# Attention with a learned position bias and a gated MLP, float32: in the bias stage, VectorE and ScalarE share the relu blocks and the copies out of PSUM, and GpSimd makes none

## The chip, the core and the metric

One core of a Trainium2 chip runs the whole program. The metric is the device time of one execution in microseconds (us). The engines are TensorE (PE in the rows; PEld is its weight load), VectorE (DVE), ScalarE (ACT), GpSimd (POOL), and SyncE (SP), which issues most DMAs. A "q" behind an engine's name is its sequencer, which issues and waits.

## What is computed

The reference is an attention block (4 batches, 8 heads, 576 positions, head dimension 64) whose scores get a bias from a small network on relative positions, followed by a gated MLP (512 to 2048 to 512) over the 2304 tokens:

```
pos = np.arange(S)
psi_rel = np.log1p(np.abs(pos[:, None] - pos[None, :]))
psi_i = np.log1p(np.maximum(pos[:, None], 1.0))
x = (psi_rel / psi_i)[..., None]
h = np.maximum(x @ w1 + b1, 0.0)
bias = h @ w2
scores = scale * np.matmul(q, k.transpose(0, 1, 3, 2)) + bias.transpose(2, 0, 1)[None]
...
g = h * np.tanh(sp)
return (g @ w_out)
```

Only the bias stage is touched: `x`, `h` and `bias` above.

## The kernel before

The program has three stages: the position bias (about the first 73 us of the trace), the attention over 16 head pairs with 5 row chunks each, and the MLP.

**The bias stage.** The bias of a row i and a column j depends on |i - j| and on i alone, so for 16 rows at a time the kernel makes a table over the distance and lets a DMA lay it out as rows. It does so in 36 turns, in the order of the list `ts` (lines 417 and 433); "turn 5" below is the sixth of that list. Each turn has

- four relu blocks `ht` (`make_h`, lines 448 to 463): `max(at + bb, 0)` over 128 partitions (4 rows x 32 hidden units) and n distances, n from 304 to 576. `maker`, a table of the engine of each block, is filled by a planner (lines 429 to 446): it keeps a sum of what each engine has spent and gives a block to the engine that would be done first, by prices per element;
- matmuls with `w2t` into a PSUM tile `bps` of 1024 columns (lines 488 to 492); there are two such tiles, so the matmuls of a turn need the tile of two turns earlier to be copied out;
- two scaled copies out of PSUM into `bt` (`evac`, lines 465 to 475): the left part, read backwards (`ps[:, left:0:-1]`), and the right part (`ps[:, :right]`). Both start at the low columns of the tile. Both are done by ScalarE here (lines 469 and 470);
- a DMA from `bt` to the bias table in DRAM, issued by SyncE (line 475). `bt` has eight buffers.

The loop (lines 482 to 512) makes the blocks of turn idx + 2, then issues the matmuls of turn idx, then the copies of turn idx - 1. GpSimd's blocks are made two turns further ahead (line 485). The engines work in the order of their instructions, so whatever stands behind a waiting instruction on the same engine waits too. ScalarE and VectorE also do the first steps of the attention in between (`SOFT_AT`): scores, add_bias (line 230, VectorE), exps (line 240, ScalarE) and norm (lines 246 and 247 on VectorE, 250 on GpSimd) of steps 0 and 1 behind turns 18 and 27, and splits of k and q (lines 174 and 179) at turns 9 and 12. GpSimd issues the 1.2 MB loads `qkhi` (line 169); line 511 is the second of these.

**Behind the stage.** The bias chunks are read back by `load_bias` (lines 182 to 193). The last one waits for the DRAM writes of the last turns; step 4 of the attention adds it (line 230).

Of the kernel before, what the change touches and what calls it, by code (L numbers as in the profile page):

```python
# [11 lines left out]
ALU = mybir.AluOpType  # L12
# [34 lines left out]
def kernel(ctx: ExitStack, tc, qk, v, wb, w2, w_in, w_out, psia, psi4, rinv, eye, out):  # L47
    nc = tc.nc
    pe, dve, act, pool, sp = nc.tensor, nc.vector, nc.scalar, nc.gpsimd, nc.sync
# [107 lines left out]
    def load_raw(i):  # L157
        hp, b = divmod(i, B)
        raw = rawp.tile([P, QW], F32, name="rawqk")
        sp.dma_start(out=raw[0:64], in_=qk[b, hp, 0:64, :QW])  # L160
        sp.dma_start(out=raw[64:128], in_=qk[b, hp, 64:128, QW:])
        vt = vp.tile([P, 2, 5, D], F32, name="vt")
        sp.dma_start(out=vt, in_=v[b, hp].rearrange("p (h c d) -> p h c d", h=2, c=5))
        qk_raw[i], v_t[i] = raw, vt

    def load_hi(i):
        hp, b = divmod(i, B)
        hi = hip.tile([P, 2 * QW], F32R, name="qkhi")
        pool.dma_start(out=hi, in_=qk[b, hp])
        qk_hi[i] = hi  # L170

    def split_k(i):
        kl = qk_hi[i][64:128, QW:]
        dve.tensor_tensor(kl, qk_raw[i][64:128], kl.bitcast(F32), op=ALU.subtract)

    def split_q(i):

        lo = q_los[i % 2]
        dve.tensor_tensor(lo[0:64], qk_raw.pop(i)[0:64], qk_hi[i][0:64, :QW].bitcast(F32), op=ALU.subtract)  # L179
        q_lo[i] = lo  # L180

    def load_bias(hp, c):
        h0, h1 = 2 * hp, 2 * hp + 1
        rows = P if c < 4 else 64
        src = bias_d[c][:, :rows * PITCH].rearrange("h (i j) -> h i j", j=PITCH)[:, :, PAD:PAD + S]
        t = bias_t[hp, c] = biasp.tile([P, 2 * S if c < 4 else S], F32, name=f"bias{c}")
        if c < 4:
            sp.dma_start(out=t[:, 0:S], in_=src[h0])
            sp.dma_start(out=t[:, S + 64:], in_=src[h1, :, 0:512])
            sp.dma_start(out=t[:, S:S + 64], in_=src[h1, :, 512:S])  # L190
        else:
            for r in range(2):
                sp.dma_start(out=t[r * 64:r * 64 + 64], in_=src[h0 + r])
# [48 lines left out]
    def norm(n):  # L242
        c = steps[n][1]
        pt, m = live[n]
        k = 2 if c < 4 else 1
        dve.tensor_scalar(m[:, 4:4 + k], m[:, 2:2 + k], 1e-9, None, op0=ALU.add)  # L246
        dve.reciprocal(m[:, 4:4 + k], m[:, 4:4 + k])  # L247
        if c < 4:
            pv = pt.rearrange("p (h s) -> p h s", h=2)
            pool.tensor_tensor(pv, pv, m[:, 4:6].unsqueeze(2).to_broadcast([P, 2, S]), op=ALU.mult)  # L250
        else:
            pool.tensor_tensor(pt[:, S:640], pt[:, 512:S], m[:, 4:5].to_broadcast([P, 64]), op=ALU.mult)
            pool.tensor_tensor(pt[:, 0:S], pt[:, 0:S], m[:, 4:5].to_broadcast([P, S]), op=ALU.mult)
# [149 lines left out]
    at = bc.tile([P, S], F32, name="at")  # L403
# [3 lines left out]
    rinv_t = bc.tile([P, S // 16], F32, name="rinv_t")  # L407
    bb = bc.tile([P, S // 4], F32, name="bb")
# [13 lines left out]
    def reach(t):  # L422

        left, right = 16 * t + 15, S - 16 * t
        n = max(left + 1, right)
        return left, right, n + n % 2


    spent = {"v": 0.0, "a": 0.0, "g": 1.1}
    maker = {}  # L430
    SOFT_AT = (18, 27, 35)
    BIAS_AT = (12, 20, 24, 32, 36)
    for idx, t in enumerate(ts):
        spent["a"] += 1.15 + (1.6 if idx in SOFT_AT else 0.0)
        spent["v"] += (1.8 if idx in SOFT_AT else 0.0) + (1.4 if idx in (9, 12) else 0.0)
        spent["g"] += 2.1 if idx - 4 in SOFT_AT else 0.0
        n = reach(t)[2]
        price = {"v": 0.13 + 0.00052 * n, "a": 0.26 + 0.00071 * n}
        if idx >= 3:
            price["g"] = 0.2 + 0.0046 * n  # L440
        for cg in (3, 2, 1, 0):
            e = min(price, key=lambda k: spent[k] + price[k])
            spent[e] += price[e]
            maker[idx, cg] = e
            if e == "g":
                del price["g"]

    def make_h(idx, engines):
        if idx >= NB:
            return  # L450
        n = reach(ts[idx])[2]
        for cg in range(4):
            e = maker[idx, cg]
            if e not in engines:
                continue
            ht = hpool.tile([P, S], F32, name="ht")
            k = 4 * ts[idx] + cg
            if e == "a":
                act.activation(ht[:, :n], at[:, :n], AF.Relu, bias=bb[:, k:k + 1])
            else:  # L460
                eng = dve if e == "v" else pool
                eng.tensor_scalar(ht[:, :n], at[:, :n], bb[:, k:k + 1], 0.0, op0=ALU.add, op1=ALU.max)  # L462
            h_t[idx, cg] = ht

    def evac(t):
        ps = bps_t.pop(t)
        bt = bo.tile([P, NW], F32, name="bt")
        left, right, _ = reach(t)
        act.mul(bt[:, :left], ps[:, left:0:-1], rinv_t[:, t:t + 1])
        act.mul(bt[:, left:], ps[:, :right], rinv_t[:, t:t + 1])  # L470

        c = t // 8
        a = (16 * t - P * c) * PITCH + PAD - 15
        dst = bias_d[c][:, a:a + 16 * (PITCH + 1)].rearrange("h (i j) -> i h j", j=PITCH + 1)
        sp.dma_start(out=dst[:, :, :NW], in_=bt)

    make_h(0, "va")
    make_h(1, "va")
    make_h(3, "g")
    load_hi(0)  # L480
    sp.dma_start(out=ident, in_=eye)
    for idx in range(NB + 2):
        if idx < NB:
            t = ts[idx]
            make_h(idx + 4, "g")
            make_h(idx + 2, "va")
            n = reach(t)[2]
            ps = bps.tile([P, 1024], F32, name="bps")
            for a in range(0, n, 512):
                for cg in range(4):  # L490
                    pe.matmul(ps[cg * 32:cg * 32 + 32, a:min(a + 512, n)], w2t,  # L491
                              h_t[idx, cg][:, a:min(a + 512, n)], start=True, stop=True)
            bps_t[t] = ps
        if 1 <= idx <= NB:
            evac(ts[idx - 1])
        if idx == 1:
            load_raw(0)
        if idx == 9:
            split_k(0)
        if idx == 12:  # L500
            split_q(0)
        if idx in BIAS_AT:
            load_bias(0, ORDER[BIAS_AT.index(idx)])
        for lag, do in enumerate((scores, add_bias, exps)):
            if idx - lag in SOFT_AT:
                do(SOFT_AT.index(idx - lag))
        if idx - 4 in SOFT_AT[:-1]:
            norm(SOFT_AT.index(idx - 4))
        if idx == 14:
            load_raw(1)  # L510
        if idx == 18:
            load_hi(1)
# [204 lines left out]
```

## Time and profile before

| what | us |
|---|---|
| median of 3 runs (784.4 to 784.8) | 784.63 |
| the profiled execution, its own time | 784.46 |
| span of that execution's trace | 782.7 |
| VectorE busy in the span | 616.9 |
| ScalarE busy in the span | 451.2 |
| GpSimd busy in the span | 327.4 |
| TensorE busy in the span | 729.7 |

The span is the time between the first and the last instruction of the program that was recorded; 1.8 us of the execution's own time lie around it. A busy share is an average over stages with different limits, so the rows below are taken from the bias stage by stretches of the span (us from its start). In rows, `out<-in` gives the tiles, then partitions x elements, `xN` the number of instructions merged into the row, and a bracket the idle time before it and what ended that. The duration of an instruction is somewhat longer than the distance to the next start on its engine, since two overlap at their ends; the distance is called its slot below.

### The profile page before, as it was taken

Reading aid. Unit: us, or ns where it says so; the run is one execution under the profiler, and the core shown is the slowest. Engines: PE = TensorE matmul, PEld = TensorE weight load, DVE = VectorE, ACT = ScalarE, POOL = GpSimd, SP = SyncE. Lnnn points to the kernel's source line nnn. Section 1 sums busy time; section 2 is a strip of 40 time slices with the busy share of each in tenths; the row PEclk is TensorE's granted clock in tenths of the full one; section 3 lists DMA queues with packets and bytes.
Section 4 is the critical chain, followed back from the end, with each engine's and each line's share of the span. In section 5 each row is a group of like instructions: output and inputs, shape, how many; then the busy total and the mean of one; then the engine's idle time right before and its main releaser. Section 6 shows DMA issues by size and latency. Waiting matters only on the chain.

```text
span 782.7 us, 11785 instructions
## 1 busy us (share of the span) xinstructions
PE 729.7 (93%) x4144; PEld 548.1 (70%) x4144; DVE 616.9 (79%) x1112; ACT 451.2 (58%) x979; POOL 327.4 (42%) x186
## 2 busy tenths in 40 slices
PE   6888999999899999989889789999999999999997
PEld 2233766766666777767667667888998888888886
DVE  7998899999999889887999997566576556665554
ACT  3656867767777777775566555444444444454443
POOL 7883777777777777763655441000000000000000
PEclk9999999999999999999899999999999999999999
DMA  6896669555966695531242212000020200010001
GB/s 180 241 315 180 203 160 295 167 175 177 297 185 171 198 289 156 155 105 43 81 145 99 80 54 81 1 1 0 33 77 1 81 0 1 1 54 1 1 0 54
DMA packets 39307, 88.81 MB, mean 113 GB/s; under 512 B 9808, under 2 KB 16464, under 8 KB 37200
## 3 DMA queue, kind: packets, MB, share of 16 engines
q1 hardware_dynamic: 36368, 67.91, 29.0%
q0 software_dynamic: 2304, 19.92, 8.1%
q8 instruction: 33, 0.54, 0.3%
q10 hardware_dynamic: 576, 0.22, 0.1%
q14 instruction: 26, 0.21, 0.1%
HBM read 67.71 MB, written 20.33 MB: 112 GB/s over the span
## 4 chain that ended last, share of the span: by engine, by line
PE 58%; DVE 22%; issue 4%; ACT 4%; DMA 3%; POOL 2%; POOLq 0%; DVEq 0%; ACTq 0%
PE y L603 20%; PE h L560 19%; PE s L217 6%; DVE pt L230 5%; PE o L298 5%; PE tp L271 5%; DVE w L120 3%; ACT pt L240 2%; DVE w L118 2%; DMA vt<-in_v_dram 2%; DVE e L567 2%; DVE e L578 1%; DVE m L246 1%; DVE ht L462 1%; DVE e L577 1%
## 5 line engine op out<-in xcount | busy, mean ns | idle before, releaser
L250 POOL TENSOR_TENSOR pt<-pt,m 128x1152 f32<-128x1152 f32 x64 | 157.2, 2457 | 60.6 <-DVE m L247 57.3
L240 ACT ACTIVATE pt<-pt,m 128x576 f32<-128x576 f32 x144 | 111.0, 771 | 72.8 <-DVE m L230 72.5
L230 DVE CUSTOM_DVE_ANT_0 pt<-s,bias 128x576 f32<-128x576 f32 x144 | 103.7, 752 | 23.4 <-PE s L217 15.8
L603 PE MATMUL y<-wlo,ghi 128*128 128x512 f32 x288 | 114.7, 398 | 5.1 <-POOL wlo L136 5.0
L603 PE MATMUL y<-who,ghi 128*128 128x512 f32 x288 | 114.5, 398 | 4.1 <-ACT ghi L583 2.4
L603 PE MATMUL y<-who,glo 128*128 128x512 f32 x288 | 114.9, 399 | 3.2 <-POOL glo L584 3.0
L583 ACT CAST ghi<-e 128x512 fp32r<-128x512 f32 x72 | 44.6, 620 | 103.9 <-DVE e L578 103.9
L565 ACT ACTIVATE e<-h 128x512 f32<-128x512 f32 x72 | 42.9, 597 | 84.2 <-PE h L560 84.2
L566 DVE TENSOR_SCALAR e<-e 128x512 f32<-128x512 f32 x72 | 33.8, 469 | 65.3 <-ACT e L565 65.3
L271 PE MATMUL tp<-ident,pt 128*128 128x128 f32 x512 | 67.0, 274 | 18.0 <-ACT main L272 18.0
L560 PE MATMUL h<-xhi,whi 128*128 128x512 f32 (+1 forms) x320 | 81.0, 375 | 1.4 <-DVE xhi L542 1.4
L560 PE MATMUL h<-xlo,whi 128*128 128x512 f32 (+1 forms) x320 | 79.9, 371 | 0.1
L560 PE MATMUL h<-xhi,wli 128*128 128x512 f32 (+1 forms) x320 | 79.3, 370 | 0.0
L217 PE MATMUL s<-qkhi 128*128 128x288 f32 x320 | 77.0, 322 | 0.7 <-DVE m L230 0.7
L298 PE MATMUL o<-main,vt 128*64 128x320 f32 (+1 forms) x512 | 75.8, 418 | 0.1
L271 PEld LDWEIGHTS tp<-ident,pt 128*128 128x128 f32 x512 | 57.3, 140 | 23.5 <-issue 23.3
L584 DVE TENSOR_TENSOR glo<-e,ghi 128x512 fp32r<-128x512 f32 x56 | 38.8, 693 | 41.3 <-ACT ghi L583 41.3
L217 PE MATMUL s<-qkhi,qlo 128*128 128x288 f32 x320 | 68.9, 297 | 0.2 <-DVE qlo L179 0.2
L491 PE MATMUL bps<-ht,w2t 128*32 128x512 f32 (+17 forms) x352 | 54.5, 507 | 15.5 <-DVE ht L462 12.3
L217 PEld LDWEIGHTS s<-qkhi 128*128 128x128 f32 x320 | 49.2, 188 | 27.7 <-DVE m L247 11.3
L272 ACT COPY main<-tp 128x512 f32<-128x512 f32 x128 | 67.5, 579 | 1.0 <-PE tp L271 1.0
L603 PEld LDWEIGHTS y<-wlo,ghi 128*128 128x128 f32 x288 | 54.5, 189 | 19.2 <-POOL wlo L136 7.2
(83 smaller groups left out, 1377.1 us busy)
## 6 DMA issues: line engine op xcount, KB each, us to landing
qkhi<-in_qk_dram POOLq DMA_DIRECT2D x16, 1216.0 KB, 8.4
bias_d<-bt SPq DMA_DIRECT2D x36, 295.5 KB, 3.9
rawqk<-in_qk_dram SPq DMA_DIRECT2D x32, 304.0 KB, 6.7
w<-in_w_in_dram SPq DMA_DIRECT2D x16, 512.0 KB, 4.3
w<-in_w_out_dram SPq DMA_DIRECT2D x16, 512.0 KB, 3.4
vt<-in_v_dram SPq DMA_DIRECT2D x16, 320.0 KB, 8.4
bias<-bias_d SPq DMA_DIRECT2D x16, 288.0 KB, 5.7
out_dram<-w SPq DMA_DIRECT2D x17, 256.0 KB, 2.3
```

The source lines that it names most:

```text
L217: pe.matmul(s[:, j, :SH], stat[:, q0:q0 + P], hi[:, QW + kc + j * SH:QW + kc + (j + 1) * SH], start=(k == 0), stop=(k == len(todo) - 1))
L230: dve.tensor_tensor_reduce(out=halves(pt[:, sl]), in0=s[:, :, :SH], in1=halves(bt[:, sl]), scale=-0.125, scalar=BIG, op0=ALU.add, op1=ALU. ...
L240: act.activation(ps, ps, AF.Exp, bias=m[:, u:u + 1], scale=-1.0, accum_out=m[:, 2 + u:3 + u])
L250: pool.tensor_tensor(pv, pv, m[:, 4:6].unsqueeze(2).to_broadcast([P, 2, S]), op=ALU.mult)
L271: pe.transpose(tp[:, k * P:(k + 1) * P], pt[:, c0:c0 + P], ident)
L272: act.copy(main[:, h, :, off:off + P], tp.rearrange("p (k q) -> p k q", k=4))
L298: pe.matmul(o[h * 64:h * 64 + 64, :w], vt[:, h, k, :], main[:, h, k, :], start=(k == 0), stop=False, **kw)
L491: pe.matmul(ps[cg * 32:cg * 32 + 32, a:min(a + 512, n)], w2t, h_t[idx, cg][:, a:min(a + 512, n)], start=True, stop=True)
L560: pe.matmul(h[:, u * n:(u + 1) * n], w["i", g4, d][:, r * P:(r + 1) * P], x[:, d, :n], start=(k == 0), stop=(k == 11))
L565: act.activation(e, h, AF.Exp)
L583: act.copy(ghi, e)
L603: pe.matmul(ys[blk][t], g[:, c0:c0 + P], w, start=(f == 0 and k == 0), stop=(f == NFC - 1 and k == 2))
```

## The change

The planner no longer knows GpSimd, gives the left and the right copy of each turn to VectorE or ScalarE as well (`taker`), and has other prices. `make_h` has no engine list any more, and the two calls for GpSimd's blocks are gone. Nothing else in the program is edited.

```
-    spent = {"v": 0.0, "a": 0.0, "g": 1.1}
-    maker = {}
+    spent = {"v": 0.0, "a": 0.0}
+    maker, taker = {}, {}
...
     for idx, t in enumerate(ts):
-        spent["a"] += 1.15 + (1.6 if idx in SOFT_AT else 0.0)
+        spent["a"] += 1.6 if idx in SOFT_AT else 0.0
         spent["v"] += (1.8 if idx in SOFT_AT else 0.0) + (1.4 if idx in (9, 12) else 0.0)
...
-        price = {"v": 0.13 + 0.00052 * n, "a": 0.26 + 0.00071 * n}
-        if idx >= 3:
-            price["g"] = 0.2 + 0.0046 * n
-        for cg in (3, 2, 1, 0):
...
+        for side, m in enumerate((left, right)):
+            taker[t, side] = least({"v": 0.1 + 0.00104 * m, "a": 0.19 + 0.00083 * m})
+        for cg in range(4):
+            maker[idx, cg] = least({"v": 0.1 + 0.00052 * n, "a": 0.19 + 0.00083 * n})
...
-        act.mul(bt[:, :left], ps[:, left:0:-1], rinv_t[:, t:t + 1])
-        act.mul(bt[:, left:], ps[:, :right], rinv_t[:, t:t + 1])
+        for side, (dst, src) in enumerate(((bt[:, :left], ps[:, left:0:-1]), (bt[:, left:], ps[:, :right]))):
+            if taker[t, side] == "a":
+                act.mul(dst, src, rinv_t[:, t:t + 1])
+            else:
+                dve.tensor_scalar(dst, src, rinv_t[:, t:t + 1], None, op0=ALU.mult)
...
-    make_h(3, "g")
...
-            make_h(idx + 4, "g")
-            make_h(idx + 2, "va")
+            make_h(idx + 2)
```

By the planner's tables, the 144 blocks stood before as 117 on VectorE (51,440 columns in all), 7 on ScalarE (3,392) and 20 on GpSimd (8,528); now 97 on VectorE (43,152) and 47 on ScalarE (20,208). Of the 72 copies, 32 (6,722 columns) go to VectorE and 40 (14,554) stay on ScalarE. In 14 turns VectorE takes the left copy and ScalarE the right (turns 0 to 4, 6, 7, 10, 13, 15, 23, 25, 31, 33), in 18 ScalarE takes the left and VectorE the right (5, 8, 11, 14, 16 to 22, 24, 26, 28 to 30, 32, 34), and in 4 ScalarE takes both (9, 12, 27, 35).

ScalarE's order before, copies of turns 3 to 6 (`bt<-bps`) and two relu blocks (`ht<-at,bb`); in brackets, the counters that an instruction waits for, each named after the engine that raises it:

```order
L469 ACTIVATE bt<-bps,rinv_t 128x63 [waits PE_49]
L470 ACTIVATE bt<-bps,rinv_t 128x528
L469 ACTIVATE bt<-bps,rinv_t 128x79 [waits PE_49]
L470 ACTIVATE bt<-bps,rinv_t 128x512
L469 ACTIVATE bt<-bps,rinv_t 128x95 [waits PE_49]
L470 ACTIVATE bt<-bps,rinv_t 128x496
L459 ACTIVATE ht<-at,bb 128x432 [waits DVE_49]
L459 ACTIVATE ht<-at,bb 128x432 [waits PE_49]
```

The left copy waits for the turn's matmuls, and the right one follows at once. ScalarE now, turns 3 to 6:

```order
L469 ACTIVATE bt<-bps,rinv_t 128x528 [waits DVE_49]
L458 ACTIVATE ht<-at,bb 128x464 [waits Activation_49]
L469 ACTIVATE bt<-bps,rinv_t 128x512 [waits DVE_49]
L458 ACTIVATE ht<-at,bb 128x448 x2
L469 ACTIVATE bt<-bps,rinv_t 128x95 [waits PE_49]
L458 ACTIVATE ht<-at,bb 128x432 [waits Activation_49]
L458 ACTIVATE ht<-at,bb 128x432
L469 ACTIVATE bt<-bps,rinv_t 128x480 [waits DVE_49]
```

ScalarE makes one or two blocks a turn, and its right copies of turns 3, 4 and 6 wait for a counter of VectorE in place of TensorE's. VectorE now, turns 4 to 6:

```order
L471 TENSOR_SCALAR bt<-bps,rinv_t 128x79 [waits PE_49]
L460 TENSOR_SCALAR ht<-at,bb 128x448 [waits DVE_49]
L460 TENSOR_SCALAR ht<-at,bb 128x448 [waits Activation_49]
L471 TENSOR_SCALAR bt<-bps,rinv_t 128x496 [waits Activation_49]
L460 TENSOR_SCALAR ht<-at,bb 128x432 [waits DVE_49]
L460 TENSOR_SCALAR ht<-at,bb 128x432
L471 TENSOR_SCALAR bt<-bps,rinv_t 128x111 [waits PE_49]
```

Copies now stand between VectorE's blocks, and its right copy of turn 5 (496 columns) waits for a counter of ScalarE. On GpSimd, the program's order up to the first norm is now:

```order
L155 MEMSET qlo_104 64x1216
L155 MEMSET qlo_105 64x1216
L169 DMA qkhi<-in_qk_dram 128x2432 x2
L250 ISA
L250 TENSOR_TENSOR pt<-pt,m 128x1152 x2
```

Both loads `qkhi` stand right behind the memsets; before, one relu block stood ahead of the first load and twelve more ahead of the second.

## Rows read from the trace of the kernel before

**Rows 1.** Busy time by stretch: us, engines (instructions), granted clock, DMA share, GB/s

```profile
0.00:5.20 5.20, 0.00 (x0) 0.00 (x0) 0.81 (x4) 1.31 (x2) 2.35 (x6) 1.00 0.37 90
5.20:71.20 66.00, 55.67 (x363) 18.50 (x364) 65.87 (x131) 37.10 (x83) 52.73 (x24) 0.97 0.80 246
```

**Rows 2.** Timeline at the end of the stage, DVE, ACT and SP: start, us, what

```profile
67.03 4.27 DVE L462 TENSOR_SCALAR ht<-at,bb 128x496 f32<-128x496 f32 x6
...
72.52 0.69 ACT L469 ACTIVATE bt<-bps,rinv_t 128x511 f32<-128x511 f32 x1
73.11 0.32 ACT L470 ACTIVATE bt<-bps,rinv_t 128x80 f32<-128x80 f32 x1
...
77.15 0.33 SPq L188 DMA_DIRECT2D bias<-bias_d  x1
80.07 0.76 DVE L230 CUSTOM_DVE_ANT_0 pt<-s,bias 128x576 f32<-128x576 f32 x1 [1.81 <-PE tp L283]
```

**Rows 3.** Timeline of DVE: relu blocks in a row while GpSimd is idle or held

```profile
38.82 2.22 DVE L462 TENSOR_SCALAR ht<-at,bb 128x560 f32<-128x560 f32 x5
48.11 0.96 DVE L462 TENSOR_SCALAR ht<-at,bb 128x320 f32<-128x320 f32 x3
```

**Rows 4.** Timelines of DVE and POOL: relu blocks beside GpSimd's work

```profile
5.18 21.88 DVE L462 TENSOR_SCALAR ht<-at,bb 128x576 f32<-128x576 f32 x38
50.18 2.25 DVE L462 TENSOR_SCALAR ht<-at,bb 128x352 f32<-128x352 f32 x1
50.11 2.12 POOL L250 TENSOR_TENSOR pt<-pt,m 128x1152 f32<-128x1152 f32 x1 [2.10 <-PE bps L491]
```

**Rows 5.** Timeline of DVE: its other work in the stage

```profile
27.09 1.42 DVE L174 TENSOR_TENSOR qkhi<-rawqk,qkhi 64x1216 fp32r<-64x1216 f32 x1
33.03 1.40 DVE L179 TENSOR_TENSOR qlo<-rawqk,qkhi 64x1216 fp32r<-64x1216 f32 x1
62.00 0.74 DVE L230 CUSTOM_DVE_ANT_0 pt<-s,bias 128x576 f32<-128x576 f32 x1
62.68 0.08 DVE L230 DVE_READ_ACCUMULATOR2_ANT m<- 128x1 f32 x1
66.75 0.16 DVE L246 TENSOR_SCALAR m<-m 128x2 f32<-128x2 f32 x1
66.94 0.17 DVE L247 RECIPROCAL m<-m 128x2 f32<-128x2 f32 x1
```

**Rows 6.** Timeline of DVE in the MLP: its copies out of PSUM

```profile
476.55 1.28 DVE L622 COPY w<-y 128x512 f32<-128x512 f32 x2
778.68 0.42 DVE L614 COPY w<-y 128x256 f32<-128x256 f32 x1
```

**Rows 7.** Timeline of ACT: copies and relu blocks

```profile
9.65 0.27 ACT L469 ACTIVATE bt<-bps,rinv_t 128x15 f32<-128x15 f32 x1 [3.71 <-PE bps L491]
9.82 0.73 ACT L470 ACTIVATE bt<-bps,rinv_t 128x576 f32<-128x576 f32 x1
10.44 0.72 ACT L459 ACTIVATE ht<-at,bb 128x512 f32<-128x512 f32 x1
...
20.04 1.20 ACT L459 ACTIVATE ht<-at,bb 128x432 f32<-128x432 f32 x2
21.13 0.35 ACT L469 ACTIVATE bt<-bps,rinv_t 128x111 f32<-128x111 f32 x1
```

**Rows 8.** Timeline of ACT: the two exps of step 0, and what follows

```profile
44.36 0.77 ACT L240 ACTIVATE pt<-pt,m 128x576 f32<-128x576 f32 x1
45.87 0.48 ACT L469 ACTIVATE bt<-bps,rinv_t 128x271 f32<-128x271 f32 x1
```

**Rows 9.** The chain that ended last, in order of time: from ACT's copy to TensorE

```profile
46.35 0.43 ACT bt L470
46.78 0.04 issue
46.82 4.14 PE bps L491 x24
```

**Rows 10.** Timelines of PE and ACT: the matmuls of turn 31 and its copy

```profile
64.58 0.96 PE L491 MATMUL bps<-ht,w2t 128*32 128x448 f32 x8 [2.21 <-DVE ht L462]
65.73 0.64 ACT L469 ACTIVATE bt<-bps,rinv_t 128x447 f32<-128x447 f32 x1 [0.41 <-ACT bt L470]
```

**Rows 11.** Busy time by stretch, as rows 1: where the granted clock fell

```profile
46.00:48.00 2.00, 1.18 (x9) 0.34 (x10) 2.00 (x4) 1.58 (x5) 2.00 (x2) 0.78 0.72 254
48.00:50.00 2.00, 2.00 (x14) 1.28 (x14) 1.97 (x9) 0.89 (x2) 0.01 (x1) 0.50 1.02 398
50.00:52.00 2.00, 1.73 (x10) 0.21 (x3) 2.00 (x2) 1.75 (x4) 1.89 (x1) 0.86 1.03 347
```

**Rows 12.** DMA issues of the stage: KB each, median us to landing; then POOL's timeline

```profile
bias_d<-bt SPq DMA_DIRECT2D x36, 295.5 KB, 3.9
7.86 0.76 POOL L169 DMA_DIRECT2D qkhi<-in_qk_dram  x1
44.33 0.58 POOL L169 DMA_DIRECT2D qkhi<-in_qk_dram  x1
```

More of the change, by code (lines that the diff above doesn't have):

```diff
@@ L426, in reach, with least, make_h @@
         return left, right, n + n % 2
-    spent = {"v": 0.0, "a": 0.0, "g": 1.1}
-    maker = {}
+    spent = {"v": 0.0, "a": 0.0}
+    maker, taker = {}, {}
     SOFT_AT = (18, 27, 35)
     BIAS_AT = (12, 20, 24, 32, 36)
+    def least(price):
+        e = min(price, key=lambda k: spent[k] + price[k])
+        spent[e] += price[e]
+        return e
     for idx, t in enumerate(ts):
-        spent["a"] += 1.15 + (1.6 if idx in SOFT_AT else 0.0)
+        spent["a"] += 1.6 if idx in SOFT_AT else 0.0
         spent["v"] += (1.8 if idx in SOFT_AT else 0.0) + (1.4 if idx in (9, 12) else 0.0)
-        spent["g"] += 2.1 if idx - 4 in SOFT_AT else 0.0
-        n = reach(t)[2]
-        price = {"v": 0.13 + 0.00052 * n, "a": 0.26 + 0.00071 * n}
-        if idx >= 3:
-            price["g"] = 0.2 + 0.0046 * n
-        for cg in (3, 2, 1, 0):
[L442 to L448, printed above, removed]
+        left, right, n = reach(t)
+        for side, m in enumerate((left, right)):
+            taker[t, side] = least({"v": 0.1 + 0.00104 * m, "a": 0.19 + 0.00083 * m})
+        for cg in range(4):
+            maker[idx, cg] = least({"v": 0.1 + 0.00052 * n, "a": 0.19 + 0.00083 * n})
+    def make_h(idx):
         if idx >= NB:
@@ L453, in make_h @@
             e = maker[idx, cg]
-            if e not in engines:
-                continue
             ht = hpool.tile([P, S], F32, name="ht")
@@ L460, in make_h @@
             else:
-                eng = dve if e == "v" else pool
-                eng.tensor_scalar(ht[:, :n], at[:, :n], bb[:, k:k + 1], 0.0, op0=ALU.add, op1=ALU.max)
+                dve.tensor_scalar(ht[:, :n], at[:, :n], bb[:, k:k + 1], 0.0, op0=ALU.add, op1=ALU.max)
             h_t[idx, cg] = ht
@@ L475, in evac @@
         sp.dma_start(out=dst[:, :, :NW], in_=bt)
-    make_h(0, "va")
-    make_h(1, "va")
-    make_h(3, "g")
+    make_h(0)
+    make_h(1)
     load_hi(0)
```

## The prediction

> **What bounds the stage now.** The busy times by stretch come first: from 5.2 to 71.2 us VectorE is busy for 65.87 of 66.00 us, ScalarE for 37.10, GpSimd for 52.73 [rows 1]. So VectorE sets the pace of the bias stage. The timeline of its end comes next: VectorE's last relu block ends at 67.03 + 4.27 = 71.30, ScalarE's last copy at 73.11 + 0.32 = 73.43, and then come the last DRAM write, the read back (issued at 77.15) and the add of that chunk at 80.07 [rows 2]. From the last copy on it is DMA latency that the change does not touch, 80.07 - 73.43 = 6.6 us, and the attention starts from there. So the question is only when the last copy ends: a microsecond there is a microsecond of the whole.
>
> **VectorE's own work.** Five blocks in a row (one of 560 columns, four of 576) take 2.22 us and three of 320 take 0.96 [rows 3]; taking off 0.08 for the end of the last, this is 0.125 + 0.00053 n us for a block of n columns (2.14 and 0.88 by that formula). The 117 blocks of before would then take 117 x 0.125 + 51,440 x 0.00053 = 41.9 us. The rest of VectorE's work is the two splits, 2.8; four adds of bias with a slot of 62.68 - 62.00 = 0.68, 2.7; and two norms of 0.3, 0.6 [rows 5]. That makes 48.0, but from 5.18 to 71.30 pass 66.1. The 18.1 us between are GpSimd's: the first 38 blocks take 21.88 us, 0.58 each, where five of the largest size go at 0.43, and one block of 352 columns takes 2.25 us where GpSimd's multiply of 2.12 us runs beside it [rows 3, 4].
>
> Now: 97 blocks, 97 x 0.125 + 43,152 x 0.00053 = 35.0. The 32 copies have no row in this stage; the nearest are VectorE's copies out of PSUM in the MLP, two of 512 columns in 1.28 us and one of 256 in 0.42 [rows 6], which gives 0.08 + 0.00102 m, so 32 x 0.08 + 6,722 x 0.00102 = 9.4. That the left parts are read backwards costs ScalarE nothing that can be seen, and I take it as free here; 0.1 us more for each would be 3.2. The other work stays, 6.1. GpSimd's 20 blocks are gone, but its two norm multiplies remain, 2.25 - 0.31 = 1.9 us each [rows 4], 3.8. The sum is 54.3 us, **11.8 less than before**.
>
> **ScalarE's.** Copy slots are 9.82 - 9.65 = 0.17 us for 15 columns and 10.44 - 9.82 = 0.62 for 576, so 0.16 + 0.0008 m; two blocks of 432 have slots of (21.13 - 20.04)/2 = 0.55, so 0.20 + 0.0008 n [rows 7]. 47 blocks make 25.6, 40 copies 18.0, two pairs of exps of 45.87 - 44.36 = 1.5 make 3.0 [rows 8]: 46.6 us. By busy time alone it fits under VectorE.
>
> **The new wait.** Before, one engine made both copies of a turn. In 32 turns now the two engines share them, and the order in the section on the change shows that the second copy does not wait for the matmuls but for a counter of the engine that makes the first: ScalarE's 528 columns of turn 3 wait for VectorE, VectorE's 496 of turn 5 for ScalarE. The two copies of a turn follow each other, across engines that each work in order. Where VectorE is second, all its later relu blocks stand behind the wait, and the matmuls of two turns later too.
>
> A handover costs what the copy runs over its slot and the wake-up of the next engine. From ScalarE that is 0.73 - 0.62 = 0.11 and 0.04 [rows 7, 9], so 0.16; from VectorE 0.08 and about as much, 0.13. From the first matmul of a turn to its copy pass 65.73 - 64.58 = 1.15 us [rows 10], and since a turn takes near 2 us, the matmuls are seldom the last. I carried both queues forward turn by turn with these prices; this is where VectorE stands:
>
> - Turns 5, 8 and 11, where a turn with VectorE first is followed by one with ScalarE first and the blocks made in between are two and two. At turn 5: after VectorE's copy of turn 4, ScalarE needs 0.13, its copy of 512 columns 0.57, two blocks of 448 at 0.56, the copy of 95 columns 0.24, and 0.16 to hand over: 2.2 us. VectorE has two blocks of 0.36 to make meanwhile, 0.7. It waits 1.5. Three times, 4.5.
> - Turns 14, 16, 24, 26 and 32, the same with three blocks on VectorE and one on ScalarE. At turn 24: 0.13 + 0.38 + 0.51 + 0.48 + 0.16 = 1.66 against three blocks of 0.33, so 0.6. Five times, 3.0.
> - Turns 20 and 29, where the exps of a step stand ahead of ScalarE's left copy. At turn 20: 1.5 + a block of 0.46 + a copy of 0.38 + 0.16 = 2.5, against VectorE's 0.16 + 0.10 + 0.88 = 1.1. Twice 1.4, 2.8. Before, this ScalarE time delayed nothing on VectorE.
> - Turn 34, where no blocks are left to make: 1.4. Turn 17, two blocks on ScalarE: 0.8. All others together 0.9.
>
> Sum of the waits: 4.5 + 3.0 + 2.8 + 1.4 + 0.8 + 0.9 = **13.4 us**. VectorE starts at 5.18 [rows 4], so its copy of turn 34 ends at 5.18 + 54.3 + 13.4 = 72.9, and ScalarE's two copies of turn 35 (0.57 and 0.22, with the matmuls' end ahead of them) end 1.1 later, at 74.0: 0.6 us later than the 73.43 of before. The gain of 11.8 is eaten by the waits.
>
> Two smaller terms. TensorE's granted clock fell to 0.78, 0.50 and 0.86 in the stretches from 46 to 52 us [rows 11], behind a lull; VectorE, which waited for nothing, lost nothing by it. Now a turn's copy waits in line behind its matmuls, so such a fall counts for some 0.4 us (two turns, a little of the 1 us that each gets longer). And both qkhi loads, before issued at 7.86 and 44.33, now start behind the memsets at about 3 us [rows 12], where the DMA share is 0.37 [rows 1]. I cost this at nothing: the stage's DMA share is 0.80 [rows 1], and a write that takes 3.9 us has eight turns until its buffer is wanted. If that cover went, ScalarE's copies would wait for `bt`.
>
> The sum: 784.46 (the profiled execution) + 0.6 + 0.4 = 785.5; the median of the runs is 0.2 above that execution, so **785.6**.
>
> **A rule against a row.** The rows of before show ScalarE alone reading these tiles, so they can't show two engines on one tile [rows 7]. The order of the changed program holds them in series, and the forecast is with it. The Trainium skill, PSUM — Partial Sum Buffer, section Specifications (TRN2), says that ScalarE and VectorE can read PSUM in parallel at full bandwidth as long as they don't collide in a bank; its section on bank collisions adds that two engines on one bank have to be kept apart by a dependency. By the first sentence alone the waits would go and the time would be that of the third rival; the second agrees with the counters in the order.
>
> **The rivals.** All turn on the sum W of VectorE's waits; the stage ends where it did before, clock included, at W = 12.4. What a measurement of this kernel can tell from no change is 0.2%, 1.6 us.
>
> 1. *Slower: ScalarE is late at every turn.* VectorE is second in 18 turns. I count on little waiting in the runs of such turns (18, 19, 21, 22, 28, 30), because ScalarE is ahead there. If it is not, because blocks and copies on ScalarE come out with gaps that its slots don't show, VectorE stands at all 18 for 1.0 us: W = 18, 5.6 us over 12.4, 790.2. It decides from W = 14.0 on, a mean of 0.78 over the 18. For it: ScalarE's load rises from 37.1 busy us to near 47, and every gap falls into a line that goes through both engines. Against: between turns 16 and 22 it has one or two blocks against VectorE's two or three.
> 2. *Faster: shorter waits.* If ScalarE's parts overlap the handovers better than the slots say, W is near 8 and the time 780.2.
> 3. *Faster: side by side.* The second copies don't really wait. Then W is under 1, VectorE is through at about 60, and with a tail like that of before (2.1 us from its last block to the last copy) the stage ends near 62, 11.4 earlier: 773. For it speaks that 11.8 us of VectorE's work are gone; against it the counters in the order.
>
> That the change does not do what it says is no rival: the order has no relu block on GpSimd and copies on both engines.
>
> **How the numbers follow.** Forecast, within 0.2% of before: 0.42. Rival 1: 0.38, nearly as much, since each thing left out of the handovers makes them longer. Rival 2: 0.13. Rival 3: 0.07. So faster 0.20, same 0.42, slower 0.38. The range goes from 780.0 (W about 8, rival 2) to 790.5 (rival 1, or 0.1 us more on each copy with the clock low for longer); it leaves out rival 3 and the far tail of rival 1.
>
> **What would show it.** Right: GpSimd has no work between 3 us and the first norm; VectorE's blocks of 576 go at 0.43 throughout; VectorE is busy for about 55 us of the stage and idle for 13, most of it ended by ScalarE's `bt` at turns 5, 8, 11, 20, 29 and 34; the last copy ends near 74 us. Wrong: copies of one turn that overlap in time on both engines (rival 3), VectorE waits at turns 18, 19, 21, 22 or 28 (rival 1), VectorE copies that take much more than 0.08 + 0.00102 m, or idle time that TensorE or a DMA ends. If the last copy ends on time and the whole differs nevertheless, the step from the stage to the attention is the wrong one.

## The result, and the profile after

The changed kernel takes 789.35 us (median of 4 runs, 789.11 to 789.73) against 784.51 for the kernel before, measured beside it (4 runs, 784.1 to 784.8): a ratio of 1.0058, 95% interval 1.0046 to 1.0070, so 4.8 us slower. The time lies in the range of 780.0 to 790.5, but the likeliest case, 785.6 and so no change, was 3.7 us too low.

Busy time by stretch of the changed kernel, columns as in [rows 1]:

```profile
5.20:71.20 66.00, 42.57 (x344) 12.88 (x344) 54.50 (x138) 44.91 (x88) 4.30 (x2) 0.83 0.75 229
```

GpSimd's 52.73 busy us have fallen to 4.30 and ScalarE's 37.10 have risen to 44.91, as told. VectorE, which was busy for 65.87 of 66.00 us [rows 1], now stands idle for 11.5 of them, and TensorE's granted clock is 0.83 in place of 0.97.

The end of the stage, timelines of ACT and then of DVE (start, us, what; the bracket is the idle time before and what ended it):

```profile
76.66 0.90 ACT L469 ACTIVATE bt<-bps,rinv_t 128x511 f32<-128x511 f32 x2 [0.19 <-PE bps L490]
84.34 0.76 DVE L230 CUSTOM_DVE_ANT_0 pt<-s,bias 128x576 f32<-128x576 f32 x1 [1.98 <-DMA bias<-bias_d]
```

The last copy ends at 76.66 + 0.90 = 77.56, where it ended at 73.43 [rows 2]: 4.13 later. The add of step 4 starts at 84.34 in place of 80.07, 4.27 later, and the span is 787.3 in place of 782.7, 4.6 longer. So nearly all of the loss is there when the stage ends, and the attention and the MLP only carry it on.

What VectorE's copies wait for, from the view of waits, 5 to 85 us (engine and line, what ended the wait: total us, times, longest):

```profile
DVE bt L471 <- ACT bt L469: 12.1, 13, 2.0
...
DVE bt L471 <- PE bps L490: 0.8, 2, 0.4
```

VectorE stands 12.1 us at its copies until ScalarE has made its own of the same turn. VectorE had no such wait before. The timeline of DVE shows where:

```profile
5.37 5.09 DVE L460 TENSOR_SCALAR ht<-at,bb 128x576 f32<-128x576 f32 x12
...
15.92 0.81 DVE L460 TENSOR_SCALAR ht<-at,bb 128x448 f32<-128x448 f32 x2
18.21 0.73 DVE L471 TENSOR_SCALAR bt<-bps,rinv_t 128x496 f32<-128x496 f32 x1 [1.49 <-ACT bt L469]
...
23.20 0.68 DVE L471 TENSOR_SCALAR bt<-bps,rinv_t 128x448 f32<-128x448 f32 x1 [1.34 <-ACT bt L469]
...
29.33 0.63 DVE L471 TENSOR_SCALAR bt<-bps,rinv_t 128x400 f32<-128x400 f32 x1 [1.31 <-ACT bt L469]
...
37.15 0.48 DVE L471 TENSOR_SCALAR bt<-bps,rinv_t 128x255 f32<-128x255 f32 x1
...
46.53 0.55 DVE L471 TENSOR_SCALAR bt<-bps,rinv_t 128x320 f32<-128x320 f32 x1 [1.22 <-ACT bt L469]
...
48.57 2.88 DVE L460 TENSOR_SCALAR ht<-at,bb 128x352 f32<-128x352 f32 x3
...
54.78 0.48 DVE L471 TENSOR_SCALAR bt<-bps,rinv_t 128x256 f32<-128x256 f32 x1 [0.50 <-ACT bt L469]
...
58.33 0.45 DVE L471 TENSOR_SCALAR bt<-bps,rinv_t 128x224 f32<-128x224 f32 x1 [0.53 <-ACT bt L469]
...
60.17 0.76 DVE L230 CUSTOM_DVE_ANT_0 pt<-s,bias 128x576 f32<-128x576 f32 x1 [0.68 <-PE s L217]
...
66.14 0.40 DVE L471 TENSOR_SCALAR bt<-bps,rinv_t 128x176 f32<-128x176 f32 x1 [1.99 <-ACT bt L469]
...
76.50 0.32 DVE L471 TENSOR_SCALAR bt<-bps,rinv_t 128x96 f32<-128x96 f32 x1 [1.58 <-ACT bt L469]
```

The six waits of over 1 us are those of turns 5, 8, 11, 20, 29 and 34; turns 24 and 26 stand for the small ones. At 60.17 the first add of bias of step 1 waits for TensorE's scores. ScalarE at turn 5, from its timeline:

```profile
16.15 0.68 ACT L469 ACTIVATE bt<-bps,rinv_t 128x512 f32<-128x512 f32 x1
16.72 1.23 ACT L458 ACTIVATE ht<-at,bb 128x448 f32<-128x448 f32 x2
17.83 0.34 ACT L469 ACTIVATE bt<-bps,rinv_t 128x95 f32<-128x95 f32 x1
```

It ends the copy of 512 columns of turn 4, makes two blocks, then the left copy of turn 5 until 17.83 + 0.34 = 18.17, and 0.04 later VectorE starts its copy of that turn. VectorE had been through with its two blocks at 16.73.

To size the terms I added up VectorE's instructions from its first block to its copy of turn 34, each from its start to the start of the next with idle time taken off. That copy ends at 76.50 + 0.32 = 76.82:

| VectorE, us | predicted | measured |
|---|---|---|
| first block starts at | 5.18 | 5.37 |
| 97 blocks, with the time beside GpSimd's multiplies | 38.8 | 40.0 |
| 32 copies | 9.4 | 11.6 |
| splits, adds, norms | 6.1 | 6.0 |
| waits | 13.4 | 13.9 |
| copy of turn 34 ends at | 72.9 | 76.8 |

### The profile page after: what moved, and what is told of

Its sections match the earlier page's. It is cut to its first block, busy times and chain, and to the rows that moved or that the text cites. A ratio compares the mean times of both kernels' runs of the same rounds, so it can differ in the third digit from the quotient of the medians.

```text
span 787.3 us, 11746 instructions
## 1 busy us (share of the span) xinstructions
PE 721.4 (92%) x4144; PEld 545.8 (69%) x4144; DVE 608.9 (77%) x1124; ACT 460.6 (59%) x987; POOL 279.2 (35%) x166
## 4 chain that ended last, share of the span: by engine, by line
PE 58%; DVE 20%; DMA 6%; ACT 5%; issue 4%; POOL 1%; DVEq 0%; SPq 0%; POOLq 0%; ACTq 0%
PE y L602 20%; PE h L559 19%; PE s L217 6%; PE o L298 5%; PE tp L271 5%; DVE pt L230 4%; DVE w L120 3%; ACT pt L240 3%; DVE w L118 2%; DMA bias<-bias_d 2%; DMA rawqk<-in_qk_dram 2%; DVE e L566 2%; DVE e L577 1%; DMA bias_d<-bt 1%; DVE m L246 1%
## 5 line engine op out<-in xcount | busy, mean ns | idle before, releaser
L240 ACT ACTIVATE pt<-pt,m 128x576 f32<-128x576 f32 x144 | 111.0, 771 | 71.2 <-DVE m L230 71.0
L583 DVE TENSOR_TENSOR glo<-e,ghi 128x512 fp32r<-128x512 f32 x56 | 38.8, 693 | 41.6 <-ACT ghi L582 41.6
L490 PE MATMUL bps<-ht,w2t 128*32 128x512 f32 (+17 forms) x352 | 43.4, 598 | 29.7 <-ACT bt L469 11.8
L217 PEld LDWEIGHTS s<-qkhi 128*128 128x128 f32 x320 | 49.6, 189 | 28.3 <-DVE m L230 10.9
L559 PEld LDWEIGHTS h<-xhi,whi 128*128 128x128 f32 x320 | 58.0, 191 | 14.6 <-DVE xhi L541 2.1
```

The source lines that it names most:

```text
L217: pe.matmul(s[:, j, :SH], stat[:, q0:q0 + P], hi[:, QW + kc + j * SH:QW + kc + (j + 1) * SH], start=(k == 0), stop=(k == len(todo) - 1))
L240: act.activation(ps, ps, AF.Exp, bias=m[:, u:u + 1], scale=-1.0, accum_out=m[:, 2 + u:3 + u])
L559: pe.matmul(h[:, u * n:(u + 1) * n], w["i", g4, d][:, r * P:(r + 1) * P], x[:, d, :n], start=(k == 0), stop=(k == 11))
```

## The experiments

Each expectation names its theories by letters. In experiments 1 to 4 and 6 they are these. A: the two engines stand in series at each turn's tile, and wait since they change places as first and second. B, a rival: TensorE, at half its clock for long in the changed kernel, is what is late. C, another: the copies are dear on VectorE wherever they stand. Experiments 5, 8 and 9 say in their own words what they test. The kernel before took 785.45 us (7 runs) beside experiments 1, 2, 4 and 6, and 784.2 (19 runs) beside 3, 5, 7 and 9, on another chip. So differences between kernels are told by their ratios to it, times 784.5. All edits are to the changed kernel unless another is named.

**1. One engine a turn.** Both copies of a turn go to one engine, so that none is handed over.

```
-        for side, m in enumerate((left, right)):
-            taker[t, side] = least({"v": 0.1 + 0.00104 * m, "a": 0.19 + 0.00083 * m})
+        m = left + right
+        taker[t, 0] = taker[t, 1] = least({"v": 0.2 + 0.00104 * m, "a": 0.38 + 0.00083 * m})
```

> The changed kernel, but the planner gives both copies of a turn to one engine: 15 turns to VectorE, 21 to ScalarE (before the edit 14 turns had VectorE's copy first, 18 ScalarE's, 4 both on ScalarE). Theory A (the second copy of a turn waits for the first on the other engine): VectorE's idle time ended by ScalarE's bt falls from 12.1 us to under 0.5, the last copy ends near 64 us in place of 77.6, the time is near 776 (774 to 779). Theory B (TensorE's low clock, at half from 31 to 35, 45 to 48, 59 to 72 us, makes the stage late): TensorE's work is the same, so the time stays at 786 to 790. Theory C (VectorE's copies are too dear, 11.6 us for 32): 30 copies stay on VectorE, so the time falls by 1 us at most, 788 or more.

Measured: 776.83 us (775.78 to 778.94), ratio to before 0.9903 (0.9879 to 0.9926), 12.2 us under the change. VectorE still makes 30 copies and 94 blocks. The last copies, and all of VectorE's waits at copies (timeline of ACT, then waits):

```profile
64.55 0.91 ACT L469 ACTIVATE bt<-bps,rinv_t 128x511 f32<-128x511 f32 x2 [4.58 <-PE bps L490]
DVE bt L471 <- PE bps L490: 1.9, 3, 0.8
```

The wait for ScalarE is gone, and the last copy ends at 65.46, 12.1 us earlier than in the changed kernel. VectorE's work is much the same, and the 12.1 us of waiting are what is gone. The sharing of copies as such isn't the fault; the sharing of one turn is. (The stretches at half clock that the expectation names are misread: in the trace they are 21 to 24, 34 to 37, 48 to 61 and 69 to 75 us.)

**2. The same copies on the same engines, VectorE's always first.**

```
-        for side, (dst, src) in enumerate(((bt[:, :left], ps[:, left:0:-1]), (bt[:, left:], ps[:, :right]))):
+        sides = ((bt[:, :left], ps[:, left:0:-1]), (bt[:, left:], ps[:, :right]))
+        for side in sorted((0, 1), key=lambda k: taker[t, k] == "a"):
+            dst, src = sides[side]
```

> The changed kernel with the same copies on the same engines, but in each shared turn VectorE's copy stands first in the program. Theory A, as a matter of which engine goes first changing from turn to turn: VectorE waits for no copy of ScalarE any more, its idle time falls from 14 us to near 3 (matmuls), ScalarE's idle time stays high, the last copy ends 7 to 9 us earlier, 780 to 783. Theory B: 787 to 790. Theory C: no change, 789.

Measured: 779.67 us (778.05 to 780.24), ratio 0.9926 (0.9908 to 0.9945), 10.4 us under the change. Views of waits and timeline of DVE:

```profile
ACT bt L471 <- DVE bt L473: 11.4, 14, 2.6
DVE bt L473 <- PE bps L492: 2.7, 5, 1.0
```

```profile
16.64 0.73 DVE L473 TENSOR_SCALAR bt<-bps,rinv_t 128x496 f32<-128x496 f32 x1
```

Turn 5's copy of 496 columns starts without a wait at 16.64, where it stood 1.49 us before. Of the two engines only ScalarE now waits for the other. The expected time was a little too high: VectorE's idle time fell by 10.0 us, from 13.9 to 3.9, and the last copy came 10.3 earlier, at 67.30, where 7 to 9 had been expected.

**3. The mirror: ScalarE's copy always first** (`!=` for `==` in that edit).

> The changed kernel with ScalarE's copy first in each shared turn, the mirror of e2. If it is the change of the first engine from turn to turn that makes VectorE wait, this is as good as e2: VectorE's waits for ScalarE's bt fall from 12.1 to 3 to 6 us, the last copy ends near 68, the time is 778 to 782. If only VectorE going first helps (VectorE must never be second), VectorE waits in all 32 shared turns and the time is 789 or more.

Measured: 781.5 us (779.66 to 784.65), ratio 0.9966 (0.9952 to 0.998), 7.2 us under the change and within what was expected. View of waits:

```profile
DVE bt L473 <- ACT bt L471: 5.5, 7, 1.6
```

VectorE is second in all 32 shared turns here, and waits less (5.5 us) than when it was second in 18 (12.1). So it isn't being second that costs most, but the change of places: after a turn in which VectorE goes first, ScalarE's right copy, its blocks and its next left copy all lie between VectorE's two copies.

**4. All copies on ScalarE again, GpSimd still without blocks.**

```
-        for side, m in enumerate((left, right)):
-            taker[t, side] = least({"v": 0.1 + 0.00104 * m, "a": 0.19 + 0.00083 * m})
+        taker[t, 0] = taker[t, 1] = "a"
+        spent["a"] += 0.38 + 0.00083 * (left + right)
```

> The changed kernel with all 72 copies on ScalarE, as before the change; the 144 relu blocks still shared by VectorE (122) and ScalarE (22), none on GpSimd. Theory A: no shared turn, no wait between copies; VectorE's blocks cost 122 x 0.125 + 53,700 x 0.00053 = 43.7 us, with 6.1 of other work and 3.8 beside GpSimd's multiplies 53.6, so VectorE is through at 59, the last copy ends near 62, the time near 774 (772 to 777). Theory B: 785 or more. Theory C: also near 774, so it is e1 and e2 that tell A from C.

Measured: 773.47 us (772.28 to 774.58), ratio 0.9851 (0.983 to 0.9871). The planner gives 122 blocks to VectorE and 22 to ScalarE; VectorE has no wait at all until the last copies, which end at 61.09.

**5. The same with 20 GpSimd blocks that nothing reads**, made two turns ahead in the turns in which the kernel before made one there.

```
+    G_AT = (3, 4, 6, 8, 9, 11, 12, 13, 15, 17, 18, 20, 21, 24, 26, 27, 28, 30, 33, 35)
+    gx = bc.tile([P, S], F32, name="gx")
...
+            pool.tensor_scalar(gx[:, :n], at[:, :n], bb[:, k:k + 1], 0.0, op0=ALU.add, op1=ALU.max)
```

> e3 with 20 relu blocks on GpSimd added back, in the turns and sizes in which the kernel before had them, into a tile that nothing reads; VectorE and ScalarE still make all 144. If GpSimd's work holds up VectorE's blocks as the 18.1 us read from the trace of before say (3.8 of it beside the two multiplies that e3 still has), VectorE's 122 blocks take about 14 us more and the time is 784 to 790. Rival (those 18 us had another cause, such as waits between VectorE's blocks): 773 to 776.

Measured: 785.36 us (784.92 to 786.75), ratio 1.0014 (1.0005 to 1.0024): 12.8 us more than without them by the ratios (11.9 by the medians), and the last copy ends at 74.45 in place of 61.09, though VectorE and ScalarE do the same work in both. VectorE's first 40 blocks, from the timeline of DVE, in experiment 4 and then here:

```profile
5.34 15.45 DVE L460 TENSOR_SCALAR ht<-at,bb 128x576 f32<-128x576 f32 x40
```

```profile
5.21 24.50 DVE L460 TENSOR_SCALAR ht<-at,bb 128x576 f32<-128x576 f32 x40
```

0.39 us a block without GpSimd, 0.61 beside it. All 122 blocks take 47.6 and 60.9 us. The expectation had about 14. GpSimd's two loads `qkhi` move as well (issued at 7.89 and 30.84 us here, both from 2.85 on in experiment 4, since they stand behind its blocks), but beside the loads of experiment 4 VectorE's blocks still take 0.39 us, so I put the difference down to GpSimd's blocks.

**6. Is TensorE's clock the loss? Three more matmuls behind most turns**, into a scores tile that nothing reads.

```
+            if idx not in (17, 18, 19, 26, 27, 28) and idx < 34:
+                junk = s_ps.tile([P, 2, 512], F32, name="s")
+                for _ in range(3):
+                    pe.matmul(junk[:, 0, :288], at[:, :P], at[:, :288], start=True, stop=True)
```

> The changed kernel with three more matmuls (128 x 288, about 0.26 us each) behind the matmuls of most turns, into a PSUM tile of the scores that is not read, to keep TensorE busy. They add to TensorE's work and to nothing that is read. Theory B: the granted clock of the stage is 1.0 in place of 0.83, and the time falls to 785 or less. Theory A and C: the clock rises too, but the time stays within 1.5 us of 789.4, since a turn's matmuls are seldom what a copy waits for (0.8 us of VectorE's idle time).

Measured: 801.24 us (799.96 to 802.62), ratio 1.0205 (1.0185 to 1.0225). Neither theory's time came. Stretches and waits:

```profile
5.20:71.20 66.00, 65.39 (x430) 33.23 (x434) 45.15 (x114) 37.96 (x72) 2.10 (x1) 1.00 0.68 199
DVE bt L471 <- PE bps L490: 8.0, 8, 1.7
```

The clock is full, but TensorE is busy for 65.39 of 66.00 us and the added matmuls stand ahead of the next turn's own. Three of them take 1.65 us, from their first start to that of the next turn's matmuls, where 0.26 each had been expected. The run can't tell the clock from that load.

**7. One added matmul in place of three** (`range(1)`).

> The changed kernel with one more matmul (128 x 288, 0.26 us) behind most turns in place of e4's three, which held the copies up themselves. If TensorE's low clock (27 us of the stage at half) costs the change its time beyond the forecast of 785.6, the clock stays higher and the time falls to 786 or 787. If not, the clock rises or not and the time is 788.5 to 791, with VectorE's wait for bt of ScalarE still near 12 us.

Measured: 791.71 us (790.47 to 793.41), ratio 1.0089 (1.0071 to 1.0108). Stretches and waits:

```profile
5.20:71.20 66.00, 53.40 (x398) 18.58 (x398) 55.02 (x138) 45.08 (x89) 4.30 (x2) 1.00 0.76 229
DVE bt L471 <- ACT bt L469: 12.7, 13, 2.8
DVE bt L471 <- PE bps L490: 1.3, 3, 0.7
```

The granted clock is 1.00 in the stretch where it was 0.83, VectorE's busy time and its waits are near those of the changed kernel (55.0 and 12.7 us against 54.5 and 12.1), and the last copy ends at 77.75 against 77.56. On balance nothing comes back in the stage. But the added matmuls cost time too (0.68 us each, and not 0.26), and the timeline of DVE tells the two apart. The copies of turns 5 and 26, the first add of step 1, and the copy of turn 29; in the changed kernel these start at 18.21, 58.33, 60.17 and 66.14:

```profile
19.22 0.73 DVE L471 TENSOR_SCALAR bt<-bps,rinv_t 128x496 f32<-128x496 f32 x1 [1.37 <-ACT bt L469]
...
59.35 0.45 DVE L471 TENSOR_SCALAR bt<-bps,rinv_t 128x224 f32<-128x224 f32 x1 [0.53 <-ACT bt L469]
...
60.43 0.75 DVE L230 CUSTOM_DVE_ANT_0 pt<-s,bias 128x576 f32<-128x576 f32 x1
...
65.42 0.40 DVE L471 TENSOR_SCALAR bt<-bps,rinv_t 128x176 f32<-128x176 f32 x1 [1.40 <-ACT bt L469]
```

Until turn 5 the added matmuls lose 1.0 us: VectorE's copies of turns 2 to 4 wait 1.3 us for matmuls, in place of 0.3. From turn 5 to turn 26 both kernels take 40.1 us, so there the low clock of the changed kernel, at half for some 17 us of them, costs nothing. From turn 26 to turn 29, where no matmul is added, the changed kernel takes 7.81 us and this one 6.07. In the changed kernel the scores of step 1 run at half clock there, VectorE's two adds wait 0.68 and 0.19 us for them, and turn 29 waits 1.99 us in place of 1.40; with the clock full the adds don't wait. So the low clock cost the changed kernel 1.7 us in these turns. The 0.7 by which this kernel is then ahead is lost at the end, where an added matmul at half clock stands ahead of those of turn 34.

The extra 2.4 us of the whole are not in the stage. The add of step 4 starts at 84.00, 0.34 earlier than in the changed kernel, and the exps stay 0.4 ahead until 236 us. From there to 311 us they lose 4.8 us, while VectorE waits for loads, as it never does there in the changed kernel (view of waits, 245 to 310 us; why the loads came late isn't known):

```profile
DVE qkhi L174 <- DMA rawqk<-in_qk_dram: 5.3, 4, 2.5
```

The profiled execution, 793.41 us, is the longest of the four. So the time of this run says nothing of the clock's price, and its rows do.

**8. What is dear about VectorE's copies? Plain copies in place of scaled ones.** The factor `rinv_t` is left out of VectorE's parts of the bias.

```
-                dve.tensor_scalar(dst, src, rinv_t[:, t:t + 1], None, op0=ALU.mult)
+                dve.tensor_copy(dst, src)
```

> VectorE's 32 copies of the bias stage are plain copies; the factor 1/psi_i is left out of those parts of the bias, so the work is the changed kernel's but for that operation. Theory A (the copies were priced from a plain copy, 256 columns in 0.42 us in the MLP, while a scaled one of 256 columns took 0.48 in the changed kernel, so the operation is what the forecast mis-sized): copies of 256 columns take about 0.42 here, 32 of them take 1.5 to 2.2 us less of VectorE's time, the last copy ends about 1 to 2 us earlier than 77.6, and the kernel takes 787.2 to 788.5 against 789.35. Theory B (the stage makes the copies slower, because TensorE writes PSUM and ScalarE reads it beside them): a copy of 256 columns stays at 0.48 and the kernel within 0.5 us of 789.35.

Measured: 788.38 us (788.01 to 789.68), ratio 1.0047 (1.0034 to 1.006) to before (785.04, 11 runs beside it). Timeline of DVE and waits:

```profile
54.24 0.42 DVE L471 COPY bt<-bps 128x256 f32<-128x256 f32 x1 [0.50 <-ACT bt L469]
DVE bt L471 <- ACT bt L469: 12.3, 14, 1.8
```

A plain copy of 256 columns takes the 0.42 us of the MLP's [rows 6], a scaled one 0.48 (the row of turn 24 above). The 32 copies take 9.6 us in place of 11.6, the waits stay, and the last copy ends at 76.09, 1.5 earlier. The stage's other traffic on PSUM doesn't make the copies dearer; the operation does. The step in the whole, about 1 us, lies within the span expected, but the intervals of the two ratios overlap (1.0046 to 1.0070 for the change), so it is the rows that carry this. The price is shown at 256 columns and in the sum of the 32 copies.

**9. A version that beats both.** Experiment 4 with the planner's prices set to the slots of [rows 3, 7] and 2.2 us put on VectorE for each of GpSimd's norm multiplies.

```
-            maker[idx, cg] = least({"v": 0.1 + 0.00052 * n, "a": 0.19 + 0.00083 * n})
+            maker[idx, cg] = least({"v": 0.125 + 0.00053 * n, "a": 0.2 + 0.0008 * n})
```

> All copies on ScalarE as in e3 (last copy at 61.1 us, VectorE busy without a gap, ScalarE idle for 10 us), with the planner's prices replaced by the slots of the rows (VectorE 0.125 + 0.00053 n, ScalarE 0.20 + 0.0008 n, copies 0.32 + 0.0008 m for both) and 2.2 us put on VectorE for each of GpSimd's two multiplies. About 10 blocks move from VectorE to ScalarE, some 0.35 us of VectorE each. Theory A (VectorE's own work is what is left): the last copy ends 2 to 3 us earlier, near 58.5, and the time is 770 to 772. Rival (ScalarE or the DRAM writes have become the limit; the DMA share was 1.0 from 20 to 40 us in e3): within 1 us of e3, 772.5 to 774.5.

Measured: 771.32 us (770.87 to 771.75), ratio 0.9828 (0.9813 to 0.9842): 13.5 us under the kernel before and 18 under the change. VectorE makes 110 blocks and ScalarE 34, and the last copies end at 59.79:

```profile
5.20:60.00 54.80, 42.19 (x378) 13.64 (x379) 49.46 (x124) 51.04 (x114) 4.29 (x2) 0.91 0.92 299
```

The two engines are now about equally busy, 49.46 and 51.04 of 54.80 us. The last copy came 1.3 us earlier than in experiment 4 and not the 2 to 3 expected, and the intervals of the two ratios overlap (0.983 to 0.9871 there), so that it beats experiment 4 is likely and not shown.

## Why the prediction was right and wrong

- **The bound: right.** VectorE's work and waits set the end of the stage, and a microsecond there is one of the whole: the last copy moved by 4.13, the step-4 add by 4.27, the span by 4.6.
- **GpSimd's hold on VectorE: right, about 1 us too high.** The prediction put 18.1 us on GpSimd, of which 3.8 stay with the two multiplies, so 14.3 on its blocks. Beside such blocks VectorE's take 13.3 us more in experiment 5 than in experiment 4, and the kernel 12.8 more. The first 12 blocks of the changed kernel take 5.09 us, 0.42 each. The price of 1.9 us for a multiply holds too: the three blocks at 48.57 take 2.88 where three of 352 columns by the formula take 1.0.
- **The waits: right in place; in sum by some luck.** Turns 5, 8 and 11 were put at 1.5 each and took 1.49, 1.34 and 1.31; turn 20, at 1.4, took 1.22; turn 34, at 1.4, took 1.58. Turn 29, at 1.4, took 1.99, but 1.40 in experiment 7, where the clock is full. Of 13.9 us in all, 12.1 were ended by ScalarE's copies; I had put down all 13.4 to them. The rest are waits for matmuls (0.8 at copies, 0.9 at the two adds of step 1) and 0.1 of short gaps. The adds' 0.9 and the 0.6 more at turn 29 are the clock's, which had no part in the 13.4; without them the sum would be 12.4. Experiments 1 to 3 show that the order of the copies makes the waits for ScalarE, not the load.
- **The step that failed: "32 x 0.08 + 6,722 x 0.00102 = 9.4" for VectorE's copies.** They took 11.6, 2.2 more, so VectorE's whole work fell by 8.5 us (from 66.1 to 57.6) and not by 11.8. This is the term of the sum that was mis-sized. I took the price from plain copies in the MLP [rows 6], but these multiply by a column, and experiment 8 shows the 0.06 us that this adds to each, 2.0 of the 2.2. The slope was right: the copy of 496 columns takes 0.25 us more than that of 256. Of what set the upper end of the range, 0.1 us more on each copy was there for the wrong reason, the backward read, while "the clock low for longer" did come. That read costs nothing that can be seen: VectorE's left copy of 255 columns (at 37.15) and its right one of 256 (at 54.78) both take 0.48 us. That the time lies in the range is so in part luck.
- **The blocks: 1.2 us too low.** A block ahead of a wait counts its whole duration, not its slot; the two of 448 columns at 15.92 take 0.81 and not 0.72. Some 14 waits at 0.08 make 1.1 us, an estimate; in experiment 2, with fewer waits, the same 97 blocks take 39.1 in place of 40.0. Together with the copies, a wait sum only 0.5 above mine, and a start 0.2 later (first blocks start between 5.12 and 5.40 in the traces here), that is the miss of the stage: 2.2 + 1.2 - 0.1 for the other work + 0.5 + 0.2 = 4.0, against 76.8 - 72.9 = 3.9 at turn 34. ScalarE's last copies came 0.7 behind that and not 1.1.
- **The clock's 0.4 us: too little.** The clock fell for far longer than I had counted on. For most of that time it cost nothing, since the engines waited for each other; in turns 26 to 29 it cost 1.7 us, by experiment 7. This is no further part of the 4.0 above: it sits there in the waits, where it makes up for waits for ScalarE that were shorter than forecast.
- **The rivals.** The slower rival gave the right time, 790.2, for the wrong reason: it wanted waits at all 18 turns where VectorE is second. The waits stayed at the turns that I had named (turn 21 waited 0.16), and it was VectorE's work that was larger, with TensorE's clock in one place. "Side by side" fell: by the first sentence cited from the Trainium skill, PSUM — Partial Sum Buffer, the time would have been 773; by its section on bank collisions two engines on one bank are kept apart by a dependency. The trace agrees with the second, with 0.04 us from the end of ScalarE's copy of turn 5 to the start of VectorE's. Whether the chip could overlap them at all wasn't tried.

The Trainium skill, Perfetto Trace Analysis, section Optimizing Scalar/DVE Operations, gives about 125 ns of overhead to a VectorE access to PSUM. With the slope of [rows 6] this makes 32 x 0.125 + 6,722 x 0.00102 = 10.9 us as an estimate: nearer to the 11.6 measured for the scaled copies than my 9.4, while the plain ones took 9.6.

## What to carry to other kernels

When two engines share the parts of one tile, look in the new order for what each second part waits for, and give the same engine the first turn every time, or the whole tile to one engine: here that was worth 7 to 12 us without any work less. When a run adds work to test a cause, compare it stretch by stretch as well as in the whole: in experiment 7 a gain of 1.7 us was hidden by what the added work lost. Price a new instruction from a row of the same operation on the same memory, not from a simpler one; 0.06 us on each of 32 copies was half of what was missed. And a gain that is real (some 12 us from taking GpSimd's blocks off) can be hidden by another part of the same change, so try the parts one at a time.

## What the runs showed of the hardware that was not expected

- **A low clock that costs nothing for most of its time.** TensorE's granted clock in the stretch from 5.2 to 71.2 us was 0.83 in the changed kernel, 0.97 in the kernel before [rows 1] and 1.00 in experiment 7. In the changed kernel it was at 0.50 (1.2 of 2.4 GHz) from 48 to 61 us, after TensorE had been waiting for the copies of earlier turns. Two stretches of the changed kernel, then one of experiment 7:

```profile
50.00:52.00 2.00, 0.07 (x4) 0.07 (x8) 2.00 (x4) 0.00 (x0) 0.94 (x1) 0.50 0.40 123
58.00:60.00 2.00, 2.00 (x13) 1.20 (x6) 1.16 (x3) 2.00 (x5) 0.00 (x0) 0.50 0.74 228
```

```profile
58.00:60.00 2.00, 1.61 (x14) 0.99 (x15) 1.47 (x5) 2.00 (x5) 0.00 (x0) 1.00 0.76 236
```

  In the first TensorE has next to nothing to do, and the clock costs nothing. In the second it is busy throughout, with matmuls of the stage and the scores of step 1, and VectorE waits for them: this is where the 1.7 us are. Here the low clock was first a sign of the waits, and then a cause of some.
- **A scaled copy costs 0.06 us more than a plain one** on VectorE at 256 columns (0.48 against 0.42 us), though both move the same data.
- **GpSimd's blocks cost VectorE 13.3 us in 122 blocks** (60.9 against 47.6 us), of which 12.8 reach the whole by the ratios; about 0.6 us for each of GpSimd's 20.
